# A quarter of the last weight load cut into transfers of 8 partitions, in a fused attention and mixture-of-experts kernel

## Chip, cores and metric

The kernel runs on one core of one Trainium2 chip, written by hand with one instruction stream for each engine and explicit semaphores. The metric is the device time of one execution in microseconds (us). The kernel before the change takes 180.34 us, the median of 3 runs (180.11 to 180.72). The profiled execution took 180.35 us, of which the profile covers a span of 178.6 us. Times inside the profile are counted from the start of that span.

## The reference

Attention with a causal window comes first, then a soft mixture of experts over all its tokens. The names are those of the reference, shortened.

```
q, k, v: (8, 8, 576, 64) f32                  # batch, heads, tokens, head size
scores = q @ k^T / 8, masked: heads 0-3 see the last 32 tokens,
         heads 4-7 every fourth of the last 128
x = (softmax(scores) @ v), as 4608 tokens x 512
logits = x @ phi                              # phi: 512 x 32 (8 experts x 4 slots)
d = softmax of logits over the tokens;  slot_input = d^T @ x       # 32 x 512
for e in range(8):                            # w1: 512 x 1024, w2: 1024 x 512, each f32
    slot_out[e] = relu(slot_input[e] @ w1[e]) @ w2[e]
out = softmax(logits over the slots) @ slot_out                    # 4608 x 512 f32
```

Sixteen weight matrices of 2 MiB each (f32) and 28 MB of q, k and v are read; 9.4 MB of result are written.

## The kernel before

**Order of the work.** Every piece of work is recorded with `op(...)` as an engine, a function, the buffers that it reads and writes, an estimated cost and a key. `Prog.schedule` then plays the program through with these costs and fixes an order for each engine; `Prog.emit` (L249) writes the instructions with the semaphore waits that follow from the buffers. Transfers on GpSimd's queue (engine "pool") keep the order in which they were recorded. The costs decide only the order. They are not waits.

**Attention.** Eight units are worked off (`NU`, a pair of batches and a half of the heads each). `load_unit` (L389) issues six transfers of 288 KB from GpSimd, which convert f32 to bf16 on the way, into one of three `stg` buffers. TensorE transposes them into `TT` (L515 to L552), makes scores, values and products (L557 to L636), and the logits and slot sums are collected along the way (L638 to L726).

**Weights.** `wload` (L413) loads one matrix as one transfer from GpSimd's queue, with conversion to bf16: 128 partitions, each a run of 4096 elements, which is 16 KB of f32 read from HBM and 8 KB of bf16 written. The destination has to be free: w10 to w16 have homes of their own in `WD`; w17 and w20 to w24 lie in the three `stg` buffers once the last units have been transposed out of them; w25, w26 and w27 (second matrix of experts 5, 6 and 7) lie in `TT`, and so are issued one after the other when the last unit has been read out of `TT` (L438 to L440, L755 to L757). w27 is the last load of the program. It carries the semaphore on which the last part of the second expert layer waits.

**After attention.** The slot inputs are folded (L766), the first expert layer runs for all experts (L783), its result is transposed (L801). The second layer (L840 to L863) runs in three groups of experts, (0,1,2,3), (4,5,6) and (7), each in two halves of the columns, into one accumulation region. Group (7) reads w27 and needs all of it. `so_sb` (L864) takes the result, and the output stage (L879 to L916) multiplies it with the tokens' weights: 36 matrix multiplications of 128 x 512, each evicted by ScalarE or VectorE (L908, L909), and eleven stores from SyncE's queue.

**Fillers.** Between 125 and 150.5 us of the planned time (`FILL`, L24), `schedule` puts matrix multiplications without use into gaps of TensorE (L918 to L933). They are part of the fixed order of TensorE's instructions, whether or not the gap is there when the program runs.

**What decides when w27 is complete.** One transfer of 128 partitions is spread over 16 DMA engines, and its semaphore is complete when all 16 have reported. All loads are on one queue, so each DMA engine works off its shares in the order of issue.

Of the kernel before, what the change touches and what calls it, by code (L numbers as in the profile page):

```python
# [109 lines left out]
class Prog:  # L110
# [6 lines left out]
    def op(self, e, fn, r=(), w=(), a=(), alloc=(), cost=0.5, key=0.0, mode="f",  # L117
           sem=None, nbytes=0, after=()):
        o = Op(e, fn, cost, key, mode)
        deps = list(after)  # L120
        for b in r:
            deps += b.ready
        for b in w:
            b.fresh()
            deps += b.prev
        for b in a:
            deps += b.prev
        seen = set()
        for d in deps:
            if d.id not in seen:  # L130
                seen.add(d.id)
                o.deps.append(d)
        for b in r:
            b.reads.append(o)
        for b in list(w) + list(a):
            b.ready.append(o)
        o.wr = [b for b in list(w) + list(a) if b.pool is not None]
        for b in list(r) + list(w) + list(a):
            if b.pool is not None and b not in o.touch:
                b.left += 1  # L140
                o.touch.append(b)
        o.alloc = list(alloc)
        o.sems = sem
        o.bytes = nbytes
        self.ops.append(o)
        return o
# [145 lines left out]
def bass_dilated_sliding_attn__then__soft_moe_slots_kernel(  # L292
# [12 lines left out]
    op = P.op  # L305
# [76 lines left out]
    b_siT, b_h, b_hT, b_so = Buf(), [Buf(), Buf()], [Buf(), Buf()], [Buf(), Buf()]  # L382

    PACE = 13.1

    def due(u, x):
        return u * PACE + x

# [24 lines left out]
    def wload(name, parts=((0, 8),)):  # L413
        ap, b = HOME[name]
        e = int(name[2:])
        src = (moe_w1 if name[:2] == "w1" else moe_w2)[e]
        c = 4 if name[:2] == "w1" else 8
        v_ = src.rearrange("(p c) f -> p c f", c=c)
        d_ = ap.rearrange("p (c f) -> p c f", c=c)
        b.parts = []  # L420
        for i, (lo, hi) in enumerate(parts):
            lo_, hi_ = lo * c // 8, hi * c // 8
            sem = DmaSem(nc, f"s_{name}_{i}")
            pb = Buf()
            for al in b.al:
                pb.prev = pb.prev + al.ready + al.reads
            o = op("pool", lambda g, lo_=lo_, hi_=hi_: [g.dma_start(d_[:, lo_:hi_], v_[:, lo_:hi_])],  # L427
                   after=pb.prev, a=[pb], cost=0.6, sem=sem, nbytes=2097152 * (hi - lo) // 8)
            b.parts.append((lo, hi, pb))
            b.ready.append(o)  # L430
# [8 lines left out]
    for i in range(3):  # L439
# [10 lines left out]
       r=[b_id0], w=[b_id], cost=1.6)  # L450
# [4 lines left out]
    def asel(t, sl, base, pat, cm):  # L455
# [7 lines left out]
       r=[b_mask[0]], w=[b_mask[1]], cost=0.6)  # L463
# [16 lines left out]
    for j in range(4):  # L480
# [3 lines left out]
           r=[b_id], w=[b_sel], cost=0.1, key=1)  # L484
        op("dve", lambda g, j=j: g.tensor_copy(fold[32 * j:32 * j + 32, :],
                                               ident[32 * j:32 * j + 32, 32 * j:32 * j + 32]),
           r=[b_id], w=[b_fold], cost=0.1, key=1)
    op("dve", lambda g: g.memset(phi_pad[:], 0.0), w=[b_phi], cost=0.4, key=1)
    for hi in range(2):
# [3 lines left out]
            r=[b_phist], w=[b_phi], cost=0.2, key=1)  # L493
    for j in range(4):
        op("dve", lambda g, j=j: g.tensor_copy(phi_pad[:, :, j, 8:12], phi_st[:, :, 28:32]),
           r=[b_phist], w=[b_phi], cost=0.1, key=1)
# [233 lines left out]
    for u in range(NU):  # L730
        for j in range(4):
            st_T(u, j)
        if u + 3 < NU:
            for n_ in W_AFTER.get(u + 2, ()):
                wload(n_)
            load_unit(u + 3)
        else:
            if u == 5:
                for n_ in W_AFTER[7]:
                    wload(n_)  # L740
            for n_ in {5: ["w17", "w20"], 6: ["w21", "w22"], 7: ["w23", "w24"]}[u]:
                wload(n_)
        for i in range(6):
            st_S(u, i)
        for g in range(4):
            st_V(u, g)
        for g in range(4):
            st_P(u, g)
        for bpar in range(2):
            for x in range(2):  # L750
                st_X(u, bpar, x)
        if u % 2:
            for bpar in range(2):
                st_L(u - 1 + bpar, u)
# [6 lines left out]
       r=[b_csum], w=[b_rcs], cost=0.1, key=K1)  # L761
# [10 lines left out]
    for hi in range(2):  # L772
# [3 lines left out]
            r=[fo], w=[b_siT], cost=0.2, key=K1)  # L776
# [6 lines left out]
    for hh in range(2):  # L783
        def pe(t, hh=hh):
            for c in range(4):
                for hi in range(2):
# [6 lines left out]
                  cost=1.8, mode="c", key=K1)  # L793
        if hh == 0:
            op("act", lambda ac: ac.activation(h_sb[:, 0:512], pair(hp)[:, 0, :], ACTF.Relu),
               r=[b_hp[0], hp], w=[b_h[0]], cost=0.65, key=K1)
        else:
            op("dve", lambda vv: vv.tensor_scalar(h_sb[:, 512:1024], pair(hp)[:, 1, :], 0.0, None,
                                                  op0=AluOp.max),
               r=[b_hp[1], hp], w=[b_h[1]], cost=0.65, key=K1)  # L800
# [28 lines left out]
    def rsum(t):  # L829
# [6 lines left out]
       after=[ffn1])  # L836
    op("dve", lambda vv: vv.reciprocal(rtok[:], bank(rs)[:, 0:N_TOK // 128]), r=[rs], w=[b_rtok],
       cost=0.2, key=K1 + 1)
# [4 lines left out]
    for es_ in ((0, 1, 2, 3), (4, 5, 6), (7,)):  # L843
        for h_ in range(2):
            def pe(t, es_=es_, h_=h_):
                for cc in range(8):
                    for e in es_:
# [11 lines left out]
                       cost=0.25 if es_ == (7,) else 0.96, mode="c",  # L859
# [4 lines left out]
    for h_ in range(2):  # L864
        sl = slice(256 * h_, 256 * h_ + 256)
        if h_ == 0:
            op("dve", lambda vv, sl=sl: vv.tensor_scalar(so_sb[:, sl], pair(sp_)[:, 0, 0:256],
                                                         rcs[:, 0:1], None, op0=AluOp.mult),
               r=[b_sp[0], b_rcs], w=[b_so[0]], cost=0.35, key=K1 + 20)
        else:  # L870
            op("act", lambda ac, sl=sl: ac.activation(so_sb[:, sl], pair(sp_)[:, 1, 0:256],
                                                      ACTF.Copy, scale=rcs[:, 0:1]),
               r=[b_sp[1], b_rcs], w=[b_so[1]], cost=0.4, key=K1 + 20)
# [5 lines left out]
    for o, (t0, n) in enumerate(TILES):  # L879
# [5 lines left out]
        for j0 in range(0, n, 2):  # L885
# [14 lines left out]
            for j in range(2):  # L900
                col = rcol[o] + (0 if split else j0 + j)

                def ev(en, po=po, ost=ost, j=j, j0=j0, split=split, col=col):
# [7 lines left out]
                   cost=0.35 if split else 0.6, key=kk)  # L911
# [4 lines left out]
            r=[ob], cost=0.1, sem=so, nbytes=262144 * n, key=K1 + 30 + o)  # L916
# [59 lines left out]
```

## Time and profile before

| what | value |
|---|---|
| time, median of 3 runs | 180.34 us (180.11 to 180.72) |
| span of the profile | 178.6 us |
| TensorE busy, share of the span | 132.6 us, 74% |
| VectorE busy, share of the span | 116.0 us, 65% |
| ScalarE busy, share of the span | 92.6 us, 52% |
| GpSimd busy, share of the span | 35.4 us, 20% |
| packets on GpSimd's DMA queue (q0) | 4608, 30.94 MB written, 83.8% of 16 DMA engines' span |
| packets on SyncE's DMA queue (q1) | 2112, 9.50 MB, 13.1% |
| packets of the instruction queue q8 | 20, 0.33 MB, 0.7% |
| last three weight loads, issued | 124.3 to 125.4 us |
| w27 complete | 151.84 us |
| first use of w27 on TensorE | 151.88 us |

The page gives for each engine how long it was busy, and in 40 slices of the span how busy it was. The chain of work that ended last is followed back from the last instruction to what released it. Two further kinds of answer are used below: the busy time in chosen stretches, which also gives the mean busy share of the 16 DMA engines (a packet counts in the stretch in which it starts), and the single DMA packets of the trace (queue, start, duration, bytes). The packets carry no number of their DMA engine.

### The profile page before, as it was taken

How to read it: one execution, taken by the hardware profiler on the slowest of the kernel's cores; microseconds unless marked ns; L12 is line 12 of the kernel's file. 1: busy time of each engine (PE TensorE's matmuls, PEld its weight loads, DVE VectorE, ACT ScalarE, POOL GpSimd, SP SyncE). 2: the span in 40 equal slices, each digit the busy share in tenths (PEclk: the TensorE clock that was granted, in tenths of full speed). 3: DMA queues.
4: the chain of work that ended last, by engine and by line, in shares of the span. 5: the costliest groups of instructions: out<-in, count | busy, mean ns of one | idle time of the engine just before them, and what ended most of it. 6: DMA issues, size and time to landing. Idle time of an engine off the chain costs nothing.

```text
span 178.6 us, 5748 instructions
## 1 busy us (share of the span) xinstructions
PE 132.6 (74%) x2582; PEld 99.1 (55%) x2588; DVE 116.0 (65%) x266; ACT 92.6 (52%) x135; POOL 35.4 (20%) x71
## 2 busy tenths in 40 slices
PE   0019789878797998998888698886899998897000
PEld 0019568657676966776876576874566474321000
DVE  6960288798479679779669767869943120799000
ACT  2004666765574895774886388577230110799000
POOL 7990600610430160440010020021100000000000
PEclk9999999999999999999999999999999999999955
DMA  5999999999999999999999999999999994399997
GB/s 81 192 223 206 222 206 214 218 211 214 215 220 211 219 206 211 221 220 214 212 216 208 216 220 209 218 216 215 216 215 215 218 215 88 114 420 422 422 413 323
DMA packets 6744, 40.80 MB, mean 228 GB/s; under 512 B 1728, under 2 KB 1728, under 8 KB 2112
## 3 DMA queue, kind: packets, MB, share of 16 engines
q0 software_dynamic: 4608, 30.94, 83.8%
q1 hardware_dynamic: 2112, 9.50, 13.1%
q8 instruction: 20, 0.33, 0.7%
q14 instruction: 4, 0.03, 0.0%
HBM read 61.93 MB, written 9.44 MB: 400 GB/s over the span
## 4 chain that ended last, share of the span: by engine, by line
DVE 30%; PE 30%; DMA 20%; ACT 7%; issue 3%; POOL 2%; DVEq 0%; POOLq 0%
DMA TT<-in_moe_w_dram 15%; DVE XB L633 10%; DVE PT L583 8%; PE ps L531 6%; DVE WD L909 5%; DMA stg<-in_v_dram 5%; ACT PT L575 5%; PE ps L593 5%; PE ps L526 4%; DVE VN L598 4%; PE ps L568 4%; PE ps L677 4%; PE ps L650 3%; PE ps L622 2%; ACT TT L550 2%
## 5 line engine op out<-in xcount | busy, mean ns | idle before, releaser
L550 ACT ACTIVATE TT<-ps 128x864 f32<-128x864 f32 x32 | 28.6, 894 | 32.6 <-PE ps L531 23.5
L575 ACT ACTIVATE PT<-ps 128x768 bf16<-128x768 f32 x48 | 36.9, 814 | 9.2 <-PE ps L568 9.0
L531 PE MATMUL ps<-ident,stg 96*64 96x96 bf16 x576 | 18.1, 226 | 17.3 <-DMA stg<-in_v_dram 12.9
L633 DVE TENSOR_TENSOR XB<-ps,RV 96x768 bf16<-96x768 f32 x32 | 30.3, 948 | 0.6
L531 PEld LDWEIGHTS ps<-ident,stg 96*64 96x64 bf16 x576 | 15.9, 125 | 18.8 <-DMA stg<-in_v_dram 12.9
L598 DVE COPY VN<-ps 128x768 bf16<-128x768 bf16 x32 | 17.5, 546 | 10.0 <-PE ps L593 9.9
L622 PE MATMUL ps<-VN,PT 128*128 128x65 bf16 x384 | 18.1, 195 | 2.5 <-DVE PT L583 1.1
L662 DVE COPY XT<-ps 128x576 bf16<-128x576 bf16 x19 | 11.3, 597 | 11.0 <-PE ps L650 10.8
L568 PE MATMUL ps<-TT 64*128 64x96 bf16 x384 | 15.9, 212 | 3.0 <-DVE VN L598 1.0
L398 POOL DMA_DIRECT2D stg<-in_q_dram x16 | 8.3, 526 | 47.0 <-PE ps L531 24.9
L593 PE MATMUL ps<-ident,TT 128*128 128x128 bf16 x192 | 17.2, 232 | 0.5 <-DVE VN L598 0.3
L622 PEld LDWEIGHTS ps<-VN,PT 128*128 128x128 bf16 x384 | 14.8, 99 | 4.9 <-DVE PT L583 1.8
L650 PE MATMUL ps<-ident,XB 96*128 96x96 bf16 x192 | 12.9, 207 | 3.7 <-DVE XB L633 3.5
L526 PE MATMUL ps<-ident,stg 96*128 96x96 bf16 x288 | 14.9, 206 | 0.2
L593 PEld LDWEIGHTS ps<-ident,TT 128*128 128x128 bf16 x192 | 11.7, 103 | 4.5 <-issue 1.3
L568 PEld LDWEIGHTS ps<-TT 64*128 64x128 bf16 x384 | 10.1, 98 | 7.0 <-ACT PT L575 1.2
L583 DVE TENSOR_TENSOR PT<-PT,mask_d 128x768 bf16<-128x768 bf16 x24 | 12.9, 546 | 0.8 <-ACT PT L575 0.4
L526 PEld LDWEIGHTS ps<-ident,stg 96*128 96x128 bf16 x288 | 13.0, 98 | 0.4 <-ACT PT L575 0.3
L583 DVE TENSOR_TENSOR PT<-PT,mask_p 128x768 bf16<-128x768 bf16 x24 | 12.7, 540 | 0.4 <-ACT PT L575 0.4
L650 PEld LDWEIGHTS ps<-ident,XB 96*128 96x128 bf16 x192 | 9.5, 98 | 6.1 <-DVE XB L633 5.2
L427 POOL DMA_DIRECT2D stg<-in_moe_w_dram x6 | 3.2, 540 | 37.7 <-PE ps L526 24.6
L895 PE MATMUL ps<-so_sb,expT 128*128 128x512 bf16 x33 | 10.1, 391 | 0.7 <-DVE WD L909 0.2
(85 smaller groups left out, 175.4 us busy)
## 6 DMA issues: line engine op xcount, KB each, us to landing
WD<-in_moe_w_dram POOLq DMA_DIRECT2D x7, 1024.0 KB, 25.7
stg<-in_moe_w_dram POOLq DMA_DIRECT2D x6, 1024.0 KB, 20.9
out_dram<-WD SPq DMA_DIRECT2D x6, 1024.0 KB, 7.2
stg<-in_q_dram POOLq DMA_DIRECT2D x16, 288.0 KB, 15.3
stg<-in_k_dram POOLq DMA_DIRECT2D x16, 288.0 KB, 17.2
stg<-in_v_dram POOLq DMA_DIRECT2D x16, 288.0 KB, 19.2
TT<-in_moe_w_dram POOLq DMA_DIRECT2D x3, 1024.0 KB, 21.7
out_dram<-stg SPq DMA_DIRECT2D x2, 1024.0 KB, 11.9
```

What stands on the lines that cost most here:

```text
L526: i_ = t.transpose(bankb2(pt, a)[:, 96 * kk:96 * kk + 96], two[:, j // 2, c, :], ident[0:96, 0:96])
L531: i_ = t.transpose(bankb2(pt, a)[64 * hx:64 * hx + 64, 96 * kk:96 * kk + 96], src[:, hx, c, :], ident[0:96, 0:96])
L550: return ac.activation(d, sv, ACTF.Copy)
L568: i_ = t.matmul(pair(sc)[:, hx, QB * x:QB * x + QB], win(u, 1, h01, blk_, bpar)[64 * hx:64 * hx + 64], win(u, 0, h01, blk_, bpar)[64 * hx: ...
L575: op("act", lambda ac: ac.activation(sbt(pt)[:, 0:768].rearrange("p (x n) -> p x n", x=2), pair(sc)[:, :, 0:384], ACTF.Exp, scale=SCALE), ...
L583: return dv.tensor_tensor(p_, p_, m.unsqueeze(1).to_broadcast([128, 2, 384]), AluOp.mult)
L593: i_ = t.transpose(bankb(pv)[:, 128 * m:128 * m + 128], win(u, 2, h01, m, bpar), ident[:, :])
L598: op("dve", lambda dv: dv.tensor_copy(sbt(vn)[:, :, :, 0:64], bankb(pv)[:, 0:768].rearrange("p (m x d) -> p m x d", m=6, x=2)), r=[pv], w= ...
L622: i_ = t.matmul(pair(po)[:, bk, 65 * po_:65 * po_ + 65], sbt(pts[i])[:, o_:o_ + 128], sbt(vn)[:, m, half, 0:65], start=True, stop=True)
L633: op("dve", lambda dv: dv.tensor_tensor(sbt(xb)[:].rearrange("p m (x h d) -> p h x m d", x=2, h=2)[:, h01], pv()[:, :, :, 0:64], sbt(rv)[: ...
L650: i_ = t.transpose(bankb(px)[:, QB * m:QB * m + QB], sbt(xb)[:, m, 128 * x:128 * x + 128], ident[0:QB, 0:QB])
L662: return en.tensor_copy(d, s_)
```

## The change

w27 is no longer one transfer of 128 partitions but nine. The first covers partitions 0 to 95 as before. The other 32 partitions are cut into four groups of 8. Each group is two transfers: one with two runs of 1984 elements in each partition (7936 bytes of f32), and one with the two runs of 64 elements (256 bytes) that are missing at the ends of these. The same bytes arrive in the same places. All nine count up one semaphore, and the last group of the second expert layer waits for the sum of them.

It is for the balance of the 16 DMA engines at the end of the load stream: a transfer of 8 partitions can be served by 8 of the 16 engines, so the pieces can give one part of the engines more of w27 than the other. The planned cost of the issuing grows from 0.6 to 0.6 + 0.14 x 32 = 5.1 us in the schedule. On TensorE, VectorE, ScalarE and SyncE the instructions stand in the same order as before; on GpSimd one transfer becomes nine.

```diff
     PACE = 13.1
+    SKEWED = {"w27": 96}
...
         b.parts = []
+        if name in SKEWED:
+            sem = DmaSem(nc, "s_" + name)
+            pb = Buf()
+            for al in b.al:
+                pb.prev = pb.prev + al.ready + al.reads
+            n0 = SKEWED[name]
+
+            def skewed(g):
+                res = [g.dma_start(d_[0:n0], v_[0:n0])]
+                dv, vv = [x.rearrange("p (x c) f -> p x (c f)", x=2) for x in (d_, v_)]
+                for r in range(n0, 128, 8):
+                    for lo, hi in ((0, 1984), (1984, 2048)):
+                        res.append(g.dma_start(dv[r:r + 8, :, lo:hi], vv[r:r + 8, :, lo:hi]))
+                return res
+            o = op("pool", skewed, after=pb.prev, a=[pb], cost=0.6 + 0.14 * (128 - n0), sem=sem,
+                   nbytes=2097152)
+            b.parts.append((0, 8, pb))
+            b.ready.append(o)
+            return
```

## The prediction

> **What bounds the kernel now.** I read the chain of work that ended last first, between 124 and 156 us:
>
> ```profile
> 124.32 1.04 POOL TT L427 x2
> 125.36 26.48 DMA TT<-in_moe_w_dram
> 151.84 0.04 issue
> 151.88 0.65 PE ps L852 x16
> 152.53 0.02 issue
> 152.56 0.48 ACT so_sb L871
> ...
> 153.51 2.85 DVE WD L909 x5
> ```
>
> The end hangs on one landing: w27 is issued at 125.36 and complete at 151.84, and TensorE takes it 0.04 us later. From there to the end it is a fixed run of evictions and stores, so a landing earlier or later by d moves the end by d, as long as nothing else becomes last.
>
> Next, the busy time in stretches around that landing (time, then PE, PEld, DVE, ACT and POOL busy, PE clock, DMA share, GB/s):
>
> ```profile
> 143.00:146.00 3.00, 2.95 (x62) 2.21 (x64) 1.08 (x5) 0.48 (x3) 0.00 (x0) 1.00 1.02 213
> ...
> 147.50:148.00 0.50, 0.50 (x10) 0.26 (x12) 0.00 (x0) 0.00 (x0) 0.00 (x0) 1.00 0.71 147
> 148.00:148.50 0.50, 0.50 (x21) 0.47 (x15) 0.00 (x0) 0.00 (x0) 0.00 (x0) 1.00 0.56 115
> ...
> 149.00:149.50 0.50, 0.50 (x18) 0.35 (x12) 0.00 (x0) 0.00 (x0) 0.00 (x0) 1.00 0.47 98
> ...
> 150.00:150.50 0.50, 0.50 (x4) 0.23 (x3) 0.00 (x0) 0.00 (x0) 0.00 (x0) 1.00 0.52 115
> 150.50:151.00 0.50, 0.50 (x4) 0.15 (x2) 0.00 (x0) 0.00 (x0) 0.00 (x0) 1.00 0.08 16
> ```
>
> The last column but one is the point. All 16 DMA engines are busy until about 147.5, then half of them until 150.5. The single packets say it sharper: w27's 16 completions land in two bunches, eight from 148.06 to 149.20 and eight from 150.57 to 151.84. Eight engines idle for 2.5 us while the last load is awaited.
>
> Why eight? On one engine the packets of a weight follow each other every 606 ns (16 KB read, 8 KB written). By chaining each packet to the one that ended as it began, I can follow sixteen engines from the first load. Their lags change only where an instruction fetch (queue q8, 16 KB, 893 to 1047 ns) cuts in: that engine then stays about 1.1 us behind. The 20 fetches visit the same eight engines in a fixed cycle, two or three times each; these are the late eight. The very latest was hit by the fetch at 146.18.
>
> Last, TensorE's timeline ahead of the landing:
>
> ```profile
> 149.58 1.19 PEld L923 LDWEIGHTS ps<-mask_p,ident 128*128 128x128 bf16 x7 [0.21 <-issue]
> 149.81 1.46 PE L923 MATMUL ps<-mask_p,ident 128*128 128x512 bf16 x6 [0.16 <-issue]
> 151.88 0.34 PEld L852 LDWEIGHTS ps<-TT,hX 128*32 128x32 bf16 x16 [1.11 <-DMA TT<-in_moe_w_dram]
> 151.88 0.62 PE L852 MATMUL ps<-TT,hX 128*32 128x256 bf16 x16 [0.61 <-DMA TT<-in_moe_w_dram]
> ```
>
> Fillers (L923) run until 151.27. They stand ahead of group (7) in a fixed order, which the change leaves as it is. TensorE idles only 0.61 us for w27: that is about the ceiling of any gain here.
>
> **What the Trainium skill says.** "DMA: Bandwidth & Descriptors", section "Why a DMA increments its semaphore by 16 and not by 1", says that the number k of engines is the largest up to 16 that divides the slowest dimension of both sides, that a transfer from GpSimd with k below 16 takes k consecutive engines from a round-robin cursor, that some plain copies instead get 16 shares of ceil(partitions/16), and that all 16 engines report whatever the shape. The trace agrees for k = 16 (16 completions for each load); it has no smaller k on this queue. By the rule, 96 partitions give 16 engines 6 each, and the pieces (16 source runs, 8 partitions) 8 engines one partition each; big, end, big, end then alternate between two halves, so that all four big ones fall on one half. "Runtime: NRT & Kernel Launch", section "Instruction fetch mechanics", gives TensorE a store of 128 KiB refilled in blocks of 16 KiB, eight blocks; the cycle of eight in the trace agrees. Neither page says which engines serve these fetches. The first page's "Specifications" put line rate at 512 bytes and up: the ends (256 bytes read, 128 written) are below; no run here shows such a transfer with conversion.
>
> **The change part by part.**
> - Removed: 2 of 8 packets of w27 on every engine, 2 x 0.606 = 1.21 us.
> - Added on the half with the big pieces: 4 partitions of two runs of 7936 bytes. By bytes 8 x 0.606 x 7936/16384 = 2.35 us; a higher bound with 0.03 us of start for each run is 2.6. Net +1.14 to +1.4 us.
> - Added on the other half: 8 runs of 256 bytes. Lower bound 0.013 us each (the 128-byte packets of the phi load took 11 to 13 ns), upper bound 0.1 us, for a partial write; I take 0.05, so 0.4 us (0.1 to 0.8).
> - Eight more completion packets on every engine, at 22 ns as in the trace: 0.18 us.
> - Issuing: eight more at the 0.53 us of the TT loads, 4.3 us on GpSimd, until about 130. Nothing is queued behind them on GpSimd, and the engines reach these descriptors only after 147.5: hidden by 17 us of queue. VectorE might be slowed by descriptor writing then; the trace shows no such effect at 124 to 126, so nothing.
> - The wait of group (7) is for 144 in place of 16: no time of its own. Queued behind it on TensorE is the rest of the kernel, which waited there before too.
>
> **If the big pieces fall on the early eight (the forecast).** The latest late engine finished w26 at 145.58; six packets 3.64 and its fetch 1.12 take it to 150.34, then 0.4 + 0.2 for the small ones: 150.94, and 0.3 from last packet to landing (as before): 151.24 (150.9 to 151.65). The latest early engine: 144.03 + 3.64 + 2.5 + 0.2 + 0.3 = 150.7. So w27 is complete near 151.24, and TensorE, free of fillers at 151.2 to 151.27, begins at about 151.28 in place of 151.88. Gain 0.6 us (0.25 to 0.8): 179.75 us, from 179.5 to 180.1. That is 0.33%, just past what can be told.
>
> **Rivals.**
> - *The big pieces fall on the late eight.* 150.34 + 2.5 + 0.2 + 0.3 = 153.3, 1.5 us later (1.3 to 1.65): 181.8 us. For it: nothing in the profile names the half, and the cursor, if nothing has moved it, stands at the first engine; TensorE's fetch engines could well be numbered first. One of them is also the very first to start a packet (2.711 us), but an early one follows 3 ns later.
> - *Late and early engines alternate in number.* Then any eight neighbours hold four late ones, and the end is late by 0.65 to 1.5 us: 181.0 to 181.8. For it: in the first load the starts of the eight late ones rise, but for one, in the order of their fetch cycle from 2.711 to 3.107, over the same range as the early ones, as if interleaved. Against it: the time from last packet to landing changes smoothly along the cycle (0.35, 0.36, 0.30, 0.31, 0.31, 0.28, 0.28, 0.29 us), as among neighbours, and the early ones keep apart (0.31 to 0.34).
> - *The runs are spread over all 16 engines.* Each then has 6 + 4 x 0.5 packets, as before, and some small ones: w27 0 to 0.4 us later, 180.3 to 180.7, about 180.5. For it: 16 source runs could count as 16. Against it: the rule needs both sides.
>
> **How the numbers follow.** The forecast case has 0.50; late half 0.23, alternating 0.15, spread 0.12. Between the early and the late half the profile decides little. I lean to the early one, and say so as a lean: what speaks for the late one (numbering, cursor) has no row behind it either, and the landing delays at least speak for two halves kept apart. The forecast case reaches 0.3% (0.54 us) in about seven of ten, so faster 0.35. Same: the rest 0.15 and nearly all of spread 0.11, so 0.26. Slower: 0.23 + 0.15 + 0.01 = 0.39. The range takes in forecast and rivals: 179.5 to 181.9.
>
> **What would show it.** Right: the 16 engines' last landings within about 1 us of each other; a DMA share near 1 until about 150; w27 complete near 151.2; TensorE's idle before L852 with hX gone, so that the fillers are last. Wrong: a stretch at a share near 0.5 that lasts to 153 (big pieces on the late half), or near 0.25 (alternating), or the old two bunches in their old places (spread). The step that most easily fails is the place of the pieces; after it, the cost of the 256-byte runs.

## The result, and the profile after

The changed kernel takes 181.43 us (median, 180.87 to 182.07) against 180.34 us (180.11 to 180.72): a ratio of 1.0062, with a 95% interval of 1.0037 to 1.0088. It is 1.1 us slower. The forecast was 0.6 us faster. Medians here are over all executions, while the ratios are of those in the fast state alone and are not quotients of these medians.

The chain of work that ended last, in the changed kernel (start us, duration us, what):

```profile
150.18 1.86 PE ps L872 x48
152.04 0.16 issue
152.19 1.46 PE ps L943 x6
153.65 0.58 PE ps L872 x16
154.23 0.02 issue
154.26 0.48 ACT so_sb L891
...
155.22 4.83 DVE WD L929 x8
```

In the kernel before, a single DMA entry of 26.48 us stood here. Now the chain runs through TensorE: group (7) (L872) begins at 153.65, after six fillers (L943), and the work behind it has moved with it. TensorE is late in this execution for a reason that experiment 1 sets apart: its granted clock fell to one half from 125.04 to 131.87. But w27 was late as well. The semaphore's counts put its completion at 152.99 (before: 151.84), so with a TensorE that was free the end would still have come 1.15 us later.

The same stretches as before (time, then PE, PEld, DVE, ACT and POOL busy, PE clock, DMA share, GB/s):

```profile
143.00:146.00 3.00, 3.00 (x72) 1.91 (x65) 0.69 (x1) 0.60 (x1) 0.00 (x0) 1.00 1.05 218
...
147.50:148.00 0.50, 0.50 (x14) 0.28 (x16) 0.00 (x0) 0.00 (x0) 0.00 (x0) 1.00 0.78 154
148.00:148.50 0.50, 0.50 (x30) 0.48 (x24) 0.00 (x0) 0.00 (x0) 0.00 (x0) 1.00 0.86 170
...
149.00:149.50 0.50, 0.50 (x24) 0.35 (x16) 0.00 (x0) 0.00 (x0) 0.00 (x0) 1.00 0.62 88
...
150.00:150.50 0.50, 0.50 (x13) 0.38 (x15) 0.00 (x0) 0.00 (x0) 0.00 (x0) 1.00 0.19 24
150.50:151.00 0.50, 0.50 (x23) 0.47 (x17) 0.00 (x0) 0.00 (x0) 0.00 (x0) 1.00 0.22 28
151.00:151.50 0.50, 0.50 (x21) 0.48 (x15) 0.00 (x0) 0.00 (x0) 0.00 (x0) 1.00 0.13 24
...
152.00:152.50 0.50, 0.34 (x5) 0.26 (x4) 0.00 (x0) 0.00 (x0) 0.00 (x0) 1.00 0.16 41
```

The share of 0.5 at 149 and 150 is gone, as intended: 0.86 at 148, 0.62 at 149, 0.19 at 150. So the data is balanced better. But a remnant of two or three engines (0.13 to 0.22) lasts to 151.34 and one engine alone to 152.44, later than any data before, which ended at 151.56 (the last line also counts a fetch of instructions at 152.27).

TensorE's timeline ahead of group (7), and GpSimd's where the new pieces are issued:

```profile
152.19 1.46 PE L943 MATMUL ps<-mask_p,ident 128*128 128x512 bf16 x6 [0.16 <-issue]
153.58 0.62 PE L872 MATMUL ps<-TT,hX 128*32 128x256 bf16 x16
```

```profile
125.41 0.53 POOL L430 DMA_DIRECT2D TT<-in_moe_w_dram  x1
125.92 4.33 POOL L434 DMA_DIRECT2D TT<-in_moe_w_dram  x8
```

Issuing costs what was predicted, 0.54 us for a piece, and ends 16 us before the first piece is moved.

The single packets show where the pieces went. Here and below a run of 1984 elements is called long, one of 64 an end, and an engine late when it is one of those that the fetches of instructions delay (the late eight of the prediction). Eight engines carry the long runs, in 313 ns for each 3968 bytes written and 2.48 us for all eight of an engine. Six of them begin between 146.51 and 147.69. Two begin at 148.85 and 149.73, and these two are late engines: the latter had an instruction fetch at 148.66. They end at 151.34 and 152.44.

The engines with the short ends have moved all their data by 150.87, yet the semaphore goes on counting: 16 counts between 151.5 and 152.36, then 152.79 and 152.99. By their times, six of the 16 fit the two late engines with long runs. On the latest of these, the completion packets at 151.17, 151.80 and 152.42 are followed by counts at 151.54, 152.15 and 152.79, and by a second one 0.2 us after each. By this the other ten come from engines whose data was long done; the last of these counts stand at 152.20 and 152.27.

One more reading serves throughout. The time of an execution less its span is about 1.75 us (1.74 before, 1.77 here), and the span less the landing of w27 is 26.76 us wherever nothing else disturbs the end (178.6 - 151.84 before). A landing can be turned into a time: the median of 181.43 stands for a landing near 152.9, by this estimate.

### The profile page after: what moved, and what is told of

It reads as the page before. It is cut to its first block, busy times and chain, and to the rows that moved or that the text cites. A ratio compares the mean times of both kernels' runs of the same rounds, so it can differ in the third digit from the quotient of the medians.

```text
span 180.3 us, 5756 instructions
## 1 busy us (share of the span) xinstructions
PE 135.3 (75%) x2582; PEld 101.1 (56%) x2588; DVE 116.0 (64%) x266; ACT 92.8 (51%) x135; POOL 39.7 (22%) x79
## 4 chain that ended last, share of the span: by engine, by line
PE 47%; DVE 30%; ACT 6%; DMA 5%; issue 4%; POOL 1%; DVEq 0%; POOLq 0%
DVE XB L653 9%; PE ps L551 8%; DVE PT L603 8%; DVE WD L929 5%; PE ps L697 5%; PE ps L613 5%; DMA stg<-in_v_dram 5%; PE ps L670 4%; PE ps L943 4%; PE ps L546 4%; DVE VN L618 4%; PE ps L588 4%; ACT PT L595 3%; PE ps L642 2%; PE ps L872 2%
## 5 line engine op out<-in xcount | busy, mean ns | idle before, releaser
L642 PE MATMUL ps<-VN,PT 128*128 128x65 bf16 x384 | 18.7, 199 | 1.9 <-DVE PT L603 0.9
L642 PEld LDWEIGHTS ps<-VN,PT 128*128 128x128 bf16 x384 | 15.3, 101 | 4.3 <-DVE PT L603 1.5
L670 PE MATMUL ps<-ident,XB 96*128 96x96 bf16 x192 | 13.4, 211 | 3.3 <-DVE XB L653 3.2
L670 PEld LDWEIGHTS ps<-ident,XB 96*128 96x128 bf16 x192 | 10.1, 100 | 5.9 <-DVE XB L653 4.5
```

The costliest lines, as they stand in the source:

```text
L642: i_ = t.matmul(pair(po)[:, bk, 65 * po_:65 * po_ + 65], sbt(pts[i])[:, o_:o_ + 128], sbt(vn)[:, m, half, 0:65], start=True, stop=True)
L670: i_ = t.transpose(bankb(px)[:, QB * m:QB * m + QB], sbt(xb)[:, m, 128 * x:128 * x + 128], ident[0:QB, 0:QB])
```

## Experiments

The two theories at the start. **Place**: the long runs fall partly on engines that the fetches have made late, and these set the end. **Pieces**: cutting a load into more transfers costs by itself. Each ratio below is to the kernel before on the same chip. "Landing" is the count that completes w27, "data" the end of its last data packet.

**1. Is it the chip or the change? `e1_before_again`** is the kernel before, unchanged.

> The kernel before, unchanged, for the granted TensorE clock of more executions. The profile of the changed kernel has a stretch of half clock from 125.0 to 131.9 us that the one profile of before does not have, and all six of its executions have a mean clock of 0.950 to 0.964 against 0.974. If that stretch belongs to the change, the clock here is 0.97 or more in every execution. If it comes and goes by itself, some executions here lie at 0.95 to 0.965 too, and their spans are no or little longer, since TensorE is not last in this kernel. Time 180.3 us either way.

180.34 us, ratio 0.9991 (0.9962 to 1.0020). In its profile TensorE's clock also falls to one half, from 153.98 for 3.41 us, and its twelve executions have a mean clock of 0.942 to 0.963, as low as the changed kernel's 0.950 to 0.964. So such stretches don't need the change. In the other profiles they last 3.41 or 6.83 us and begin at 45, 77, 100, 122 to 125 or 152 to 156 us, or there is none before the last 13 us. The half clock at 125.04 in the profile after began before the first added piece was issued (125.92). One thing stays open: a stretch that begins between 122.4 and 125.1 stands in twelve of the sixteen profiles with a cut w27 and in none of the four with a whole one. The landing varied too: 152.23 here, against 151.84. The fetches come at other moments in each execution and make other engines the latest.

**2. Pieces without imbalance: `e2_even`.** The last 32 partitions go in eight transfers of 16 partitions, a quarter of the columns each.

```diff
-                for r in range(n0, 128, 8):
-                    for lo, hi in ((0, 1984), (1984, 2048)):
-                        res.append(g.dma_start(dv[r:r + 8, :, lo:hi], vv[r:r + 8, :, lo:hi]))
+                for r, s, lo, hi in tuple((r, r + 16, c, c + 512) for r in (96, 112) for c in range(0, 2048, 512)):
+                    res.append(g.dma_start(dv[r:s, :, lo:hi], vv[r:s, :, lo:hi]))
```

> The last 32 partitions of w27 in eight transfers of 16 partitions (two runs of 512 elements each), so that all 16 DMA engines get the same. As many issues on GpSimd as in the changed kernel, without the skew. If the place of the big pieces made the change slow, w27 is complete within 0.5 us of before (151.8 to 152.4) and the time is 180.3 to 180.9. If the eight more issues (and a half clock that comes with them) made it slow, the time is 181 or more and the clock 0.965 or less, as in the changed kernel.

181.13 us, ratio 1.0020 (1.0001 to 1.0039). Landing 152.55, data 152.29. Nine transfers with data behind almost every completion cost 0.2%, about a third of the loss. The landing comes 0.27 us after the data, as with a whole w27 (0.26 to 0.28), so no completions are left over at the end. Whether the 0.2% is the completions between the data or the shorter runs isn't separated.

**3. Another eight engines: `e3_shift2`, `e4_shift14`, `e9_flip`.** A short transfer of 2 or of 14 partitions ahead of the pieces moves the long runs to the places from 2 or from 14 on. In e9 each end goes ahead of its long runs, which moves these to the places from 8 on. A place is a DMA engine as GpSimd's queue counts them, from where it stood behind w26. e3 has one transfer more than the changed kernel, e4 two; e9 has as many.

```diff
-                for r in range(n0, 128, 8):
-                    for lo, hi in ((0, 1984), (1984, 2048)):
-                        res.append(g.dma_start(dv[r:r + 8, :, lo:hi], vv[r:r + 8, :, lo:hi]))
+                for r, s, lo, hi in ((96, 98, 1984, 2048), (96, 104, 0, 1984), (104, 112, 1984, 2048),
...
+                                     (120, 128, 1984, 2048), (120, 128, 0, 1984), (98, 104, 1984, 2048)):
+                    res.append(g.dma_start(dv[r:s, :, lo:hi], vv[r:s, :, lo:hi]))
```

> As the changed kernel, but the first end transfer has 2 partitions and comes ahead of the first big one, so that all big ones start 2 DMA engines further on (the other 6 partitions of that end come last). By the packets of the changed kernel six early and two late engines serve the big pieces. If the late engines are eight neighbours, a shift of 2 makes it either eight early ones (w27 complete near 151.2, 179.7 us) or four and four (w27 complete as in the changed kernel, 153 us, or a little later, about 181.5). If the place of the pieces doesn't matter, 181.4 as the changed kernel. If a transfer of 2 partitions doesn't move the cursor by 2, as the changed kernel or the flipped order.

> The same with a shift of 14, that is of 2 in the other direction (first an end transfer of 14 partitions; the last big one is shortened to two runs of 1856, and its missing columns are further end transfers of 8, so that the cursor stands after the program where it stood before). Of this and the shift by 2, one should give the big pieces to the eight early engines: w27 complete near 151.2 us, time 179.7; the other four and four, about 181.5. If the place doesn't matter, both 181.4.

> The changed kernel with each end ahead of its long pieces, so that the long runs fall on places 8 to 15 (six of them with fetches) and the ends on 0 to 7. By the place theory: long runs that begin late on six engines and on two engines early; latest end of a 3968-byte packet 152.4 to 153.1 and w27 complete at 153.0 to 153.7, as late as or up to 0.6 us later than in the changed kernel, since the latest engine counts and not their number; time 181.4 to 182.3. If the place did not matter: six early and two late as in the changed kernel and the same time within 0.2 us.

| | us | ratio | engines with long runs that are late | landing |
|---|---|---|---|---|
| changed | 181.43 | 1.0062 (1.0037 to 1.0088) | 2 of 8 | 152.99 |
| e3_shift2 | 181.97 | 1.0060 (1.0036 to 1.0083) | 3 of 8 | 153.35 |
| e4_shift14 | 181.90 | 1.0046 (1.0010 to 1.0081) | 2 of 8 | 153.39 |
| e9_flip | 181.91 | 1.0093 (1.0067 to 1.0119) | 6 of 8 | 153.21 |

None of these four windows of eight neighbours was free of late engines, and no eight neighbours can give the counts 2, 3, 2 and 6, so the idea that the late engines are one half fell. With six in place of two the landing hardly moved, so the latest engine seems to count more than their number. e9 also shows the place by itself: its ends and their completions lie ahead of the long runs, the landing comes only 0.33 us after the last data (152.88), and it is the slowest of the four by its ratio, from four executions.

**4. Which places are late? `e5_map`** adds to the kernel before a row of small transfers to free space, each with its own length, so that a packet's size names its place.

```diff
...
+    def probe(g):
+        scr = TTf[:, 12288:13376].rearrange("p (x f) -> p x f", x=2)
+        src = moe_w2[7].rearrange("(p x c) f -> p x (c f)", x=2, c=4)
+        res, r = [], 0
+        for w, n in enumerate((2,) * 8 + (3,) + (2,) * 7 + (15,), 1):
+            res.append(g.dma_start(scr[r:r + n, :, 0:32 * w], src[r:r + n, :, 0:32 * w]))
+            r += n
+        return res
...
```

> The kernel before, and behind w27 seventeen small transfers of different sizes into a part of TT that nothing uses: eight of 2 partitions, one of 3, seven of 2, one of 15 (two runs of 32 to 544 elements in each partition). They add no result and leave none out. Each packet's size tells from which transfer it is, and so which of the sixteen chains of packets stands at which place of the cursor; the fetches of 16 KB tell which chains are the late ones. Theory of two halves: eight late chains at places 0 to 7 or 8 to 15 (the changed kernel already speaks against it, with two late ones among the first eight). Neighbours, turned: eight late ones in a row somewhere, with 2 of them in places 0 to 7. Scattered: late ones in several groups, with 2, 3 and 2 late in the windows of eight from places 0, 2 and 14 on, as the packets of the changed kernel and of the two shifts have it. If a transfer of 2 partitions doesn't take two neighbours from a cursor, the pairs of the second half don't overlap with those of the first by one chain each. Time as before, or up to 1 us longer, since the stores start with the small transfers done.

180.61 us beside 180.53, one execution each. A transfer of n partitions in two runs takes n consecutive places, and the next one goes on from there. The late places are 5, 6 and 9 to 14; early are 0 to 4, 7, 8 and 15. The pair of 704 bytes (places 5, 6) came at 151.21 and 151.29, that of 768 bytes (7, 8) at 148.02 and 148.24. The window from 0 holds two late places, from 2 three, from 14 two, from 8 six: the four rows of the table above. By this map every window of eight holds at least two.

**5. All long runs on early places: `e6_early8`, with controls.** Pieces of 2, 6, 7 and 15 partitions let every long run fall on 15, 0 to 4, 7 or 8, and every end on the places between. e7 is e6 without the last seven fillers, e8 the kernel before without them.

```diff
+                B, B2 = (0, 1984), (0, 1920)
+                E, E2 = (1984, 2048), (1920, 1984)
+                for r, s, (lo, hi) in (
+                        (96, 111, E), (96, 102, B), (111, 113, E), (102, 104, B), (112, 118, E2),
...
+                        (120, 126, B2), (126, 128, E2), (126, 128, B2), (121, 128, E)):
+                    res.append(g.dma_start(dv[r:s, :, lo:hi], vv[r:s, :, lo:hi]))
```

```diff
-FILL = (125.0, 150.5)
+FILL = (125.0, 147.0)
```

> The same bytes in runs of nearly 8 KB, but the transfers are ordered and cut (2, 6, 7, 15 partitions) so that every long run falls on one of the eight places 15, 0 to 4, 7 and 8 of the cursor, which the run with marked sizes showed to be free of instruction fetches, and every 128-byte end fills the places between. If the place of the long runs is what failed in the prediction: no 3968-byte packet after about 150.3 us, all 16 engines done within about 1.3 us of each other, w27 complete 0.3 to 0.9 us ahead of the kernel before on this chip, and the time 0.2 to 0.6 us below it (fillers on TensorE end near 151.3 and bound the gain). If pieces and their completions cost by themselves, or if TensorE is bound by something else: w27 may be early, but the time is equal to or above the kernel before, by the 0.4 us that the sixteen-engine transfers cost.

> e6_early8 with the last seven filler multiplications of TensorE left out, those that end at 151.27 us in the profile before. If the fillers bound the gain once w27 is early: a further 0.1 to 0.5 us below e6_early8. If not, equal to e6_early8 within 0.2 us, or above it if a shorter run of fillers lowers the clock.

> The kernel before with the same seven fillers left out and no piece. If the landing of w27 alone sets the end: equal to the kernel before within 0.2 us, so that whatever e7_early8_nofill gains beyond this is due to the transfers. If the fillers delay the end in executions whose TensorE is late (the half-clock stretch of the changed kernel's profile): 0.1 to 0.4 us below.

e6: 183.67 us, ratio 1.0182 (1.0168 to 1.0195), the slowest so far. e7: 183.50, 1.0164 (1.0142 to 1.0185). e8: 180.62, 1.0007 (0.9988 to 1.0026), so leaving the fillers out changed nothing that can be told. The chain of e6 and its stretches (columns as above) show what happened:

```profile
134.65 19.19 DMA TT<-in_moe_w_dram
153.85 0.04 issue
153.89 0.65 PE ps L877 x16
```

```profile
149.00:150.00 1.00, 1.00 (x23) 0.61 (x16) 0.00 (x0) 0.00 (x0) 0.00 (x0) 1.00 0.67 72
150.00:151.00 1.00, 1.00 (x6) 0.43 (x5) 0.00 (x0) 0.00 (x0) 0.00 (x0) 1.00 0.29 31
151.00:152.00 1.00, 0.40 (x2) 0.00 (x0) 0.00 (x0) 0.00 (x0) 0.00 (x0) 1.00 0.01 0
152.00:153.00 1.00, 0.00 (x0) 0.00 (x0) 0.00 (x0) 0.00 (x0) 0.00 (x0) 1.00 0.00 0
```

The data did what the place theory asked: the last packet ended at 151.11 (151.56 before). But the landing came at 153.85, 2.7 us later. In this time no packet of the load stood on any engine, not even one of its completion packets, the last of which began at 151.11 (share 0.01, then 0.00; one engine was still busy with a fetch that had begun at 150.16 and took 2.02 us), and from 151.4 on TensorE stood still. From 151.0 on, the semaphore still counted 49, 33, 25, 17, 11 and 6 completions in successive half microseconds. Eighteen transfers, the main part and seventeen pieces, report from all 16 engines (288 counts). The third theory, **completions**: those of one engine are handled one after the other and pile up when no data lies between them. "DMA: Bandwidth & Descriptors" of the Trainium skill, section "Why a DMA increments its semaphore by 16 and not by 1", calls the completion of each engine a strongly ordered write that lands only after the engine's data; the order agrees with the trace (before: last data at 151.56, landing at 151.84).

**6. The price of completions: `e10_early5`, `e11_early5_cut`, `e12_early5_nofill`.** e10 has four transfers: 96 partitions, 25 meant for places 0 to 4, 7, and the ends of the 25. e11 cuts the 7 partitions into sixteen pieces of columns. e12 is e10 without the last fillers. From e10 to e11:

```diff
                 res.append(g.dma_start(dv[96:121, 0:4064], vv[96:121, 0:4064]))
-                res.append(g.dma_start(dv[121:128], vv[121:128]))
+                for i in range(0, 4096, 256):
+                    res.append(g.dma_start(dv[121:128, i:i + 256], vv[121:128, i:i + 256]))
                 res.append(g.dma_start(dv[96:121, 4064:4096], vv[96:121, 4064:4096]))
```

> Main part of 96 partitions, then 25 partitions on the five places 0 to 4 (no instruction fetches there; five packets of some 8 KB each), then 7 partitions on places 5 to 11, then the 64-byte ends of the 25: four transfers in all, so four completions on each engine in place of the seventeen of e6_early8, whose last data packet ended at 151.11 but whose last completion was seen at 153.85. Theory A (completions of one engine are handled one after the other, 0.16 to 0.2 us each, and delay the landing when they pile up without data between them; the place theory holds for the data): last data packet near 150.9 to 151.3, w27 complete 0.3 to 0.6 us after it, that is 0.2 to 0.8 us ahead of the kernel before on this chip, time 0.2 to 0.6 us below it. Theory B (the place of the data does not matter to the landing, or uneven loading costs by itself): w27 and time equal to or above the kernel before.

> e10_early5 with the transfer of 7 partitions cut into sixteen column pieces of 512 bytes written, so that the same bytes come with 19 completions on each engine in place of 4 and every engine has seven such small packets. Theory A: last data packet within 0.5 us of e10_early5 but w27 complete 2 to 3.3 us after it, near 153.3 to 154, time 1.5 to 3 us above e10_early5. If completions were free at 22 ns, as the prediction had it: 15 x 0.022 = 0.33 us later than e10_early5.

> e10_early5 with the last seven filler multiplications of TensorE left out. If w27 lands ahead of the end of the fillers (151.27 in the profile before) they bound the rest of the gain: 0.1 to 0.4 us below e10_early5. If w27 is still what TensorE waits for: equal within 0.2 us.

e10: 180.90 us, ratio 1.0016 (0.9996 to 1.0037), data 151.91, landing 152.40. e11: 184.24 us, 1.0168 (1.0116 to 1.0221), data 152.57, landing 155.48. e12: 181.04, 1.0033 (1.0014 to 1.0053), no gain. The gain expected of e10 failed to come because its 25 partitions did not go to five places: the ends lie in the trace as twelve pairs and one single, two to an engine on thirteen engines. That is the exception which the section just named states, 16 shares of ceil(partitions/16), here two each. Late engines got shares too: the last one moved two of these long packets behind its six of the main part. In e11 two chains of sixteen 512-byte packets lie at the very end, from 150.92 and 151.21: such pieces of a single run returned to the same places each time.

The price is clear nonetheless. Between data and landing lie 0.49 us in e10 with 4 completions on each engine and 2.91 us in e11 with 19: 2.42 / 15 = 0.16 us each. The last four counts of e11 come at 154.986, 155.151, 155.317 and 155.483, one every 0.166 us. The small packets are not the reason: the engine whose data ended last, at 152.57, has none of 512 bytes. Nor is a slow fetch: one ran from 151.08 to 153.10, but on another engine, for the last one was moving packets of 8128 bytes at 151.13 and 151.73. Again the engines stand idle, but for that fetch (e11, stretches):

```profile
152.00:153.00 1.00, 0.31 (x2) 0.00 (x0) 0.00 (x0) 0.00 (x0) 0.00 (x0) 1.00 0.04 2
153.00:154.00 1.00, 0.00 (x0) 0.00 (x0) 0.00 (x0) 0.00 (x0) 0.00 (x0) 1.00 0.00 0
154.00:155.00 1.00, 0.00 (x0) 0.00 (x0) 0.00 (x0) 0.00 (x0) 0.00 (x0) 1.00 0.00 0
```

**7. Completions ahead of the data.** `e13_early8_front` is e6 and `e16_after_front` the changed kernel, each with its pieces issued ahead of the main part. `e14_front5` uses whole rows only: 5, 5, 5 and 1 partitions ahead of 112, which gives places 0 to 4 ten packets of 8192 bytes and all the others 7 in place of 8. The single row came as 16 packets of 512 bytes, one on each engine. e15 is e14 without the last fillers.

```diff
-                res = [g.dma_start(d_[0:n0], v_[0:n0])]
+                res = []
...
+                res.append(g.dma_start(d_[0:n0], v_[0:n0]))
                 return res
```

```diff
...
+                res = [g.dma_start(d_[r:s], v_[r:s]) for r, s in ((0, 5), (5, 10), (10, 15), (15, 16), (16, 128))]
```

> e6_early8 with its sixteen pieces issued ahead of the main part of 96 partitions instead of behind it: same bytes, same places, same 18 completions on each engine, but now 6 packets of 0.6 us follow the last small piece. If pile-up of completions is what made e6_early8 late (data done at 151.11, landing at 153.85): landing within 0.5 us of the last data packet, near 151.2 to 151.7, time 0.2 to 0.7 us below the kernel before, 3 us below e6_early8. If the late landing came from the number of completions wherever they stand: still 153 or later and a time near 183.5.

> The changed kernel with its eight pieces ahead of the main part. Places as in the changed kernel: long runs on six early and two fetching engines. By the place theory the two fetching engines with long runs keep the end: last data packet 151.9 to 152.6, landing 0.3 us later at 152.2 to 152.9, time 0 to 0.6 us below the changed kernel but still 0.3 to 1 us above the kernel before. If piled-up completions alone made the changed kernel slower: landing near 151.3 and a time at or below the kernel before.

> Whole rows only: 5, 5, 5 and 1 partitions ahead of the main part of 112. Such single-run transfers stood on fixed first places in e11_early5_cut, so places 0 to 4 get 10 packets of 8192 bytes (place 0 11) and all others, the fetching ones among them, 7 in place of 8. By the place theory: last data packet of the fetching engines 0.62 us earlier than in the kernel before, landing near 151.1 to 151.5, time 0.3 to 0.6 us below the kernel before. If TensorE or anything else sets the end there: within 0.2 us of the kernel before.

> e14_front5 with the last seven fillers left out. If the fillers (ending at 151.27 in the profile before) bound e14_front5: 0.1 to 0.3 us below it. If the landing still does: equal within 0.2 us.

| | us | ratio | data | landing |
|---|---|---|---|---|
| e13_early8_front | 182.78 | 1.0116 (1.0083 to 1.0148) | 152.31 | 152.62 |
| e16_after_front | 180.98 | 1.0013 (0.9988 to 1.0038) | 151.28 | 151.60 |
| e14_front5 | 180.26 | 0.9991 (0.9971 to 1.0011) | 151.46 | 151.72 |
| e15_front5_nofill | 180.17 | 0.9981 (0.9961 to 1.0001) | 151.56 | 151.82 |

The wait after the data fell to 0.3 us in all four. That shows the pile-up. e13 missed its forecast of a gain all the same: its data ended 1.2 us later than e6's. On eight of its engines the first 8192-byte packet behind the pieces took 1.90 to 2.29 us in place of 0.625. They began between 145.79 and 146.74 and took about equally long, so each seems to have waited on its own engine: seventeen completions in a row are not free ahead of data either. Besides, its TensorE was late, with a half clock from 124.91 to 131.73, and group (7) began at 154.49, 1.9 us after the landing. How its loss divides between these stays open.

e16 missed a forecast too: by the place theory its data was to end at 151.9 to 152.6, and it ended at 151.28.

e14 fits the place theory in the one form that adds little else. Beside e1, whose last engine had finished w26 at the same moment (147.38 and 147.37), the landing is 0.51 us earlier, where one packet of 0.606 us was taken away. Its time, though, can't be told from the kernel before.

**8. Both orders on one chip: `e17_after_again`, `e18_after_front2`.** The changed kernel and e16 once more.

> The changed kernel once more, beside e18 on one chip. If the pile-up behind its short ends belongs to the order of its pieces: again 0.4 to 0.9% above the kernel before, landing at 152.2 or later, and the last completions of the engines without long runs more than 1 us after their last data packet. If its first profile was an unlucky phase of the fetches: a landing near 151.6 to 152.0 and a time within 0.3% of the kernel before.

> e16_after_front once more, on the same chip. If the order of the pieces (and with it the pile-up) carries most of the loss: 0.5 to 1.1 us below e17_after_again, within 0.3% of the kernel before. If the place of the long runs carries it: within 0.3 us of e17_after_again.

e17: 181.30 us, ratio 1.0036 (1.0017 to 1.0055). e18: 181.19 us, ratio 1.0000 (0.9978 to 1.0023). The chains at the landing, e17 and then e18:

```profile
126.62 26.76 DMA TT<-in_moe_w_dram
153.38 0.04 issue
153.43 0.65 PE ps L872 x16
```

```profile
127.33 25.37 DMA TT<-in_moe_w_dram
152.70 0.04 issue
152.75 0.65 PE ps L873 x16
```

The changed kernel is slower again, and here its chain does hang on w27, for TensorE is free: the late start of the first profile was not needed for the loss. A part of this landing may belong to this execution alone: between 146.2 and 147.3, packets of the main part took up to 1085 ns on many engines, which the profile after doesn't show. Twice the order with the pieces first brings the ratio back to about 1 (1.0013, 1.0000), with the long runs on the same places. So over many executions the order carries much of the loss.

One profile alone doesn't show this. In e16 and e18 too the two late engines with long runs are the last, and the landing moved from 151.60 to 152.70 between them: their long runs end at 147.50 and 147.61 in e16, at 148.57 and 148.71 in e18, about one fetch later (the prediction took 1.12 us for one). With the pieces last the landing is 152.99 or 153.38, and only 0.55 us of it lie behind the data, against 0.32 with the pieces first. What the order takes away may be a floor. The fastest executions of the changed kernel take 180.87 and 180.64 us, those with the pieces first 180.06 and 180.05. By the reading above these stand for landings of 152.4 and 152.1, and of 151.5. The counts of engines without long runs, which end at 152.27 in the profile after, would keep the changed kernel late even where the fetches fall well. This is an inference from the fastest times; the exact shares can't be read from these runs.

## Why the prediction was wrong

The forecast needed two things to hold, and neither did.

*"If the big pieces fall on the early eight (the forecast)": the place was wrong.* The late engines are not one half of the sixteen that eight neighbours make up, but places 5, 6 and 9 to 14 (experiment 4). The half from 0 holds six early ones and two late. On the later of the two a fetch cut in at 148.66, the long runs began at 149.73 and ended at 152.44: that is the landing of 152.99. In e17 also they end last (152.84, landing 153.38). The prediction named the place as the step that most easily fails, but its cases were halves, alternation, or even spread. Two late engines in eight were between them, and one is enough.

*"Eight more completion packets on every engine, at 22 ns as in the trace: 0.18 us": this term was mis-sized by seven times.* The 22 ns are how long the 4-byte packet shows on its engine. The counts of one engine follow each other every 0.165 us when no data lies between. For the eight that is 1.3 us. The profile after bears this out: the last main packet there ended at 150.62; 150.62 + 0.3 + 8 x 0.165 = 152.24, and the last counts that don't fit the two late engines with long runs came at 152.20 and 152.27. With this term the forecast's own sum becomes 150.34 + 0.3 + 1.32 = 151.96 in place of 151.24, against 151.84 before. By this sum the change would have gained nothing even with every long run on an early engine. e6 shows that case at its extreme: data earlier, landing 2.7 us behind it.

In the profile after, either failure would have been enough: without the pile-up the latest long runs give 152.44 + 0.28 = 152.72, without the late long runs the other counts end at 152.27, both behind 151.84. (0.28 is the wait from data to landing before; both are estimates.)

What held: a landing moves the end one for one (span less landing 26.76 us before, 26.76 to 26.77 in e14, e16, e17 and e18). Long runs cost 2.48 us (2.35 to 2.6 predicted). The ends were cheap, 31 ns a run (0.05 taken), and done by 150.87 (150.94 predicted). The pieces alternate between the two halves, as the same section of the Trainium skill has it: eight engines carry the long runs. Issuing is hidden. The ceiling of 0.6 us was not put to the test: the earliest landing against its like was e14's, 0.51 us ahead of e1.

The rival *"Late and early engines alternate in number"* had the right size (181.0 to 181.8) and, in a weaker form, the right picture: any eight neighbours hold late engines. It reached this size with completions at 0.2 us, though, as every case of the prediction did, so that is in part luck. It was also the rivals and not the forecast that put 181.43 inside the range of 179.5 to 181.9. The evidence set against it, landing delays that change smoothly along the cycle, did not show that the late engines are one half.

"Wrong" was to show as a stretch at a share near 0.5 or 0.25 that lasts to 153. It showed as 0.13 to 0.22, which is two or three engines of sixteen, and then one.

## What to carry to other kernels

Count a load's completions as work: each transfer on GpSimd's queue reports from all 16 engines, here 0.165 us each in series once the data has run out. Small transfers behind the last data that something waits for are the dear ones. A few ahead of the large one did better here (e16, e18); seventeen cost there too (e13). Before giving some engines more than others, find out which ones are late, with packets whose size names their place; and look at the time between last data packet and landing: here an idle DMA share with a waiting consumer was such a queue of completions. Here no version beat the kernel before by more than can be measured; the best was e15, at 0.9981 (0.9961 to 1.0001).

## What the runs showed of the hardware

- The fetches of TensorE's instructions, 16 KB each and some 0.9 to 1.1 us on the engine, fall on places 5, 6 and 9 to 14 as GpSimd's queue counts them. Their moment changes between executions and with it the landing of the last load (151.84, 152.03 and 152.23 for loads left whole).
- A fetch slows down beside a pile of small transfers: 1964 ns in e5, 2020 in e6, 2866 in e7, 1653 and 2019 in e11, against 881 to 1235 otherwise. So does a data packet directly behind such a pile: 1.90 to 2.29 us on eight engines in e13 in place of 0.625.
- Completions of one engine without data between them are counted one every 0.165 us (e11), while most of the 4-byte packets themselves take 7 to 22 ns.
- Transfers of two runs in each partition go on from place to place. Single-run ones in e10, e11 and e14 were dealt out by whole shares, on the same engines each time.
- TensorE's clock falls to one half for 3.41 or 6.83 us at moments that differ between executions, in the kernel before too. If that comes while TensorE has little slack, as from 125.04 in the profile after and 124.91 in e13, group (7) can begin after the landing (153.65 and 154.49). If it comes behind the landing, the end is later for the same landing: 26.95 to 27.97 us of span in place of 26.76 (e1, e3, e4, e6, e8 and e10 among others).
